# Adding the global keys' share of batch 0's first outputs by short matmuls from the picked rows, and sending those rows into the value tile by DMA

## The chip, the core and the metric

The kernel runs on one core of a Trainium2 chip. The metric is the device time of one execution, in microseconds (us). The kernel was already tuned: TensorE is busy in 97% of its span. A trace belongs to one execution. Traces start at the first instruction, so their spans are some 1.8 us shorter than the device times.

## The reference

Longformer attention, then a feed-forward block with a squared ReLU. Each query attends to the keys within 32 places of it and to eight global tokens; a global token attends to all and is attended by all.

```python
batch, n_heads, seq, head_dim = (8, 8, 576, 64); n_global = 8; window = 32
scores = scale * np.matmul(q, k.transpose(0, 1, 3, 2))
mask = (abs(pos[:, None] - pos[None, :]) <= window) | is_global[:, None] | is_global[None, :]
attn = softmax(np.where(mask, scores, -1e9))            # shortened
x = (attn @ v).transpose(0, 2, 1, 3).reshape(B * S, H * D)   # 4608 x 512
h = np.maximum(x @ w_in, 0.0)                            # w_in 512 x 2048
return (h * h) @ w_out                                   # w_out 2048 x 512
```

## The kernel before

The batches are worked through one after the other, and the expert matmuls (L543, L524 and L587, the two products of the feed-forward block) of one batch fill TensorE beside the attention of the next. Batch 0 has nothing to hide behind. Its heads are treated in four pairs, its 576 queries in two halves. A value tile `vb[b]` holds up to 120 keys in each of five tiles, and rows 0 to 7 of each tile are the eight global keys' values. For batch 0 these rows are picked from the tile itself with one-hot matrices `oh`, rounded to `gv16`, and copied into all five tiles before any output can be computed:

```python
def pick_values():
    gp = pst("mm", [P, 512])[0:NG]
    for x in range(NT):                                   # five matmuls of 512 columns
        nc.tensor.matmul(gp..., oh[:, x, :], vb[0][:, x, 0 : 2 * H : 2], start=(x == 0), stop=(x == NT - 1))
    dve.tensor_copy(out=gv16, in_=gp...)

def spread_values(b, op, tiles=range(NT)):
    for x in tiles:
        op(out=vb[b][0:NG, x, 0 : 2 * H : 2], in_=gv16)

# ... the program's order in batch 0, from the third pair's scores on
half0(2)                                                  # scores of pair 2, exponentials
half0(3)
pick_values()
spread_values(0, dve.tensor_copy, range(0, 4))
spread_values(0, act.copy, range(4, NT))
masked(0, ets[2], WIN)
masked(0, ets[3], WIN)
# ... DMAs of w_in, of batch 1 and of w_out; GpSimd's casts of global rows (next_in_place)
keep_warm(SCHED["w7"])                                    # four multiplications of zeros
half0_out(0, "mm"); half0_out(1, "sc"); half0_out(2, "acc"); half0_out(3, "mm")   # four lines in the file
```

`half0_out` computes a pair's outputs and denominators (L670), then `finish_outputs` takes Ln and Exp of the denominators on ScalarE (`rec`, L702 and L703) and multiplies on VectorE into `xT` (L732), which the expert matmuls read. After the four pairs come the first `scatter` of the global queries (L751), later the outputs of the second half, and a second scatter.

The softmax here doesn't subtract the row's maximum and nothing guards it: scores larger than these inputs give would overflow.

## Time and profile before

| | before |
|---|---|
| device time, median of 3 | 326.77 us (326.56 to 326.85) |
| profiled execution | 327.83 us, span 326.0 us |
| TensorE busy | 316.8 us, 2434 matmuls |
| first expert matmul starts | 25.79 us |
| clock granted to TensorE | 1.00 |

TensorE doesn't lose its clock once it has it: the page's line of the granted clock has a 9, the highest digit, in each of the forty slices of the span. (The line doesn't show the slow start: four zero matmuls at 3.47 us took 1.89 us, four at 17.08 took 1.04.) The lines of the chain and of TensorE's own timeline are in the prediction. One thing matters for all that follows: the profiled execution took 327.83 us, one microsecond over the median.

### The profile page before, as it was taken

The numbers are of one execution on the slowest core, as the hardware profiler recorded it, in microseconds if no ns is written. First come the engines' busy times: TensorE is split into PE (matmuls) and PEld (weight loads), VectorE is DVE, ScalarE is ACT, GpSimd is POOL, SyncE is SP. The second block draws the span as 40 slices with busy tenths as digits, with TensorE's granted clock in tenths as the row PEclk, the third lists the DMA queues.
The fourth block names the chain that finished last, engine by engine and source line by source line (L and its number), as shares of the span: only waits on it lengthen the run. The fifth ranks groups of instructions, "written<-read, shape, count | busy, mean of one in ns | idle before, by whom it ended". The sixth has DMA issues, their size and how long they took to land.

```text
span 326.0 us, 6920 instructions
## 1 busy us (share of the span) xinstructions
PE 316.8 (97%) x2434; PEld 164.5 (50%) x2434; DVE 227.0 (70%) x674; ACT 214.4 (66%) x418; POOL 110.2 (34%) x148
## 2 busy tenths in 40 slices
PE   6998999999999999999999999999999999999996
PEld 2645775445555455455545544454455544444444
DVE  7786987677878875987598758885888675313421
ACT  6677985569954995499549954995499636404600
POOL 9824663639800870089107700680000000000000
PEclk9999999999999999999999999999999999999999
DMA  8999999999994999399959996999610011011012
GB/s 186 176 204 190 174 186 167 154 147 107 153 131 141 73 138 171 134 83 139 132 162 82 148 126 144 98 134 132 139 60 0 34 58 39 2 73 56 2 54 75
DMA packets 148229, 37.53 MB, mean 115 GB/s; under 512 B 136171, under 2 KB 143715, under 8 KB 148195
## 3 DMA queue, kind: packets, MB, share of 16 engines
q0 software_dynamic: 105168, 17.93, 78.9%
q1 hardware_dynamic: 42880, 19.04, 30.3%
q8 instruction: 19, 0.31, 0.4%
q10 hardware_dynamic: 146, 0.13, 0.1%
q14 instruction: 16, 0.12, 0.1%
HBM read 37.30 MB, written 17.05 MB: 167 GB/s over the span
## 4 chain that ended last, share of the span: by engine, by line
PE 88%; DVE 7%; ACT 2%; issue 1%; DMA 1%
PE mm L587 29%; PE mm L524 26%; PE tr L524 9%; PE tr L587 7%; PE sc L679 3%; PE acc L679 3%; PE sc L627 3%; PE mm L543 2%; PE acc L627 2%; DVE xT L751 2%; PE tr L197 1%; DVE vb L457 1%; PE sc L670 1%; DVE xT L732 1%; ACT rec L702 1%
## 5 line engine op out<-in xcount | busy, mean ns | idle before, releaser
L587 PE MATMUL mm<-w_out,gt 128*128 128x512 f16 x448 | 104.4, 379 | 0.0
L524 PE MATMUL mm<-xT,w_in 128*128 128x512 f16 x384 | 90.8, 379 | 0.5 <-DVE xT L751 0.5
L587 PEld LDWEIGHTS <-gt 128*128 128x128 f16 x560 | 52.4, 98 | 58.6
L524 PEld LDWEIGHTS <-w_in 128*128 128x128 f16 x512 | 47.5, 98 | 53.7 <-issue 0.8
L529 ACT ACTIVATE rl<-mm 128x512 f16<-128x512 f32 x96 | 54.3, 599 | 26.7 <-PE mm L524 26.7
L530 DVE TENSOR_TENSOR gt<-rl 128x512 f16<-128x512 f16 x128 | 51.0, 422 | 17.0 <-ACT rl L529 15.6
L636 ACT ACTIVATE et<-sc 128x880 f16<-128x880 f32 (+1 forms) x32 | 29.0, 907 | 44.1 <-PE sc L627 39.1
L643 DVE TENSOR_TENSOR et<-et,mask 128x880 f16<-128x880 f16 (+1 forms) x64 | 38.9, 615 | 24.1 <-ACT et L636 23.8
L113 POOL DMA_DIRECT2D vb<-in_v_dram x40 | 40.7, 1532 | 9.0 <-DMA w_in<-in_moe_w_in_dram 7.3
L524 PE MATMUL tr<-xT,w_in 128*128 128x512 f16 x128 | 33.0, 380 | 0.0
L564 DVE COPY ot<-mm 128x512 f32<-128x512 f32 (+1 forms) x29 | 19.7, 680 | 18.0 <-PE mm L587 16.3
L636 ACT ACTIVATE et<-acc 128x880 f16<-128x880 f32 (+1 forms) x32 | 29.1, 909 | 1.0 <-PE acc L627 1.0
L703 ACT ACTIVATE rec<-rec 128x288 f32<-128x288 f32 x64 | 28.3, 443 | 2.0
L732 DVE TENSOR_TENSOR xT<-sc,rec 64x288 f16<-64x288 f32 (+1 forms) x55 | 25.0, 455 | 6.5 <-ACT rec L703 6.2
L732 DVE TENSOR_TENSOR xT<-acc,rec 64x288 f16<-64x288 f32 (+1 forms) x55 | 25.0, 455 | 3.9 <-ACT rec L703 1.1
L404 POOL DMA_DIRECT2D scr_k<-in_k_dram x30 | 26.6, 1111 | 2.8 <-issue 2.8
L679 PEld LDWEIGHTS <-vb 128*128 128x128 f16 x288 | 21.3, 98 | 11.5
L930 POOL COPY pin<-gsh 1x1 f32<-1x1 f32 x5 | 0.9, 177 | 76.4 <-DVE gsh L720 76.4
L702 ACT ACTIVATE rec<-sc 64x288 f32<-64x288 f32 (+1 forms) x55 | 22.3, 406 | 6.2 <-PE sc L679 4.2
L404 POOL DMA_DIRECT2D scr_q<-in_q_dram x24 | 25.1, 1585 | 3.0 <-DMA w_out<-in_moe_w_out_dram 3.0
L587 PE MATMUL tr<-w_out,gt 128*128 128x512 f16 x112 | 25.3, 379 | 0.0
L702 ACT ACTIVATE rec<-acc 64x288 f32<-64x288 f32 (+1 forms) x55 | 22.2, 404 | 2.0 <-PE acc L670 1.1
(147 smaller groups left out, 308.5 us busy)
## 6 DMA issues: line engine op xcount, KB each, us to landing
out_dram<-ot SPq DMA_DIRECT2D x35, 256.0 KB
vb<-in_v_dram POOLq DMA_DIRECT2D x32, 120.0 KB, 11.3
scr_q<-in_q_dram POOLq DMA_DIRECT2D x24, 144.0 KB, 5.9
scr_k<-in_k_dram POOLq DMA_DIRECT2D x24, 120.0 KB, 4.2
w_in<-in_moe_w_in_dram POOLq DMA_DIRECT2D x4, 512.0 KB, 11.9
w_out<-in_moe_w_out_dram POOLq DMA_DIRECT2D x4, 512.0 KB, 12.3
natk<-in_k_dram POOLq DMA_DIRECT2D x3, 288.0 KB, 10.9
natq<-in_q_dram POOLq DMA_DIRECT2D x3, 288.0 KB, 15.8
```

Of the source, the lines that this page charges most:

```text
L113: pool.dma_start(out=vb[b][NG : NG + KN[x], x, 2 * hs.start : 2 * hs.stop : 2], in_=v[b, hs, x * KT : x * KT + KN[x]].rearrange("h s d -> ...
L404: pool.dma_start(out=scr[(nm, b % 2)][x * pitch + off : x * pitch + off + hi - lo].rearrange("s (h d) -> s h d", d=D), in_=src[nm][b, :, l ...
L524: nc.tensor.matmul(ph, w_in[:, t, u * P : (u + 1) * P], xT[:, t, XOFF + c * TC : XOFF + (c + 1) * TC], start=(t == 0), stop=(t == NDM - 1),)
L529: nc.scalar.activation(out=rl, in_=ph, func=AF.Relu)
L530: nc.vector.tensor_tensor(out=gts[c][:, u, :], in0=rl, in1=rl, op=ALU.mult)
L587: nc.tensor.matmul(po, gts[c][:, f, m * P : (m + 1) * P], w_out[:, f, :], start=(f == 0), stop=(f == NFF - 1),)
L636: act.activation(out=et[:, :, 0:W], in_=sc[:, :, 0:W], func=AF.Exp, bias=0.0, scale=scale)
L643: dve.tensor_tensor(out=et[:, :, 0:W], in0=et[:, :, 0:W], in1=mask[:, MB[half] : MB[half] + W].unsqueeze(1).to_broadcast((P, 2, W)), op=AL ...
L679: nc.tensor.matmul(banks[e][:, o : o + w], vtf[:, t, vo : vo + P], et[:, e, so : so + w], start=(n == 0), stop=(n == nw - 1), skip_group_c ...
L702: act.activation(out=rec[r], in_=av[xs][rs, :, 0:GTOK], func=AF.Ln)
L703: act.activation(out=rec, in_=rec, func=AF.Exp, scale=-1.0)
L732: dve.tensor_tensor(out=xT[r, hp, x0 : x0 + HS].rearrange("p (k x) -> p k x", k=2), in0=av[x][r, :, 0:GTOK], in1=rec[r], op=ALU.mult,)
```

## The change

The intent is to take the copies of `gv16` out of the relay. The first half's outputs are computed from tiles whose rows 0 to 7 are still zero, and the global keys' share is added by 24 short matmuls that contract only the eight rows of `gv16`. The second half needs rows in tiles 2 to 4 alone, and gets them by three DMAs. Denominators don't need values, so pair 0's Ln may start before the share is added. The picks are split in two, and the first three windows of pair 0's outputs are put between the scores of pairs 2 and 3.

```diff
+    def pick_values(part):                    # half of the heads, 256 columns
...
+    def send_values():
+        for x in range(2, NT):
+            nc.sync.dma_start(out=vb[0][0:NG, x, 0 : 2 * H : 2], in_=gv16)
...
+    def global_keys(i, half, et, banks, wins):
...
+                nc.tensor.matmul(
+                    banks[0][D * e : D * e + D, lo_ - half * BANKC : hi_ - half * BANKC],
+                    gv16[:, 2 * hp + e], et[0:NG, e, off + lo_ : off + hi_],
+                    start=False, stop=(n == len(own) - 1), skip_group_check=True,
+                )
...
+    first = [pst("mm", [P, 512]), pst("tr", [P, 512])]
+    column_outputs(0, 0, ets[0], first, WIN, slice(0, 3))
     half0(3)
...
-    pick_values()
-    spread_values(0, dve.tensor_copy, range(0, 4))
-    spread_values(0, act.copy, range(4, NT))
     masked(0, ets[2], WIN)
-    masked(0, ets[3], WIN)
+    pick_values(0)
+    pick_values(1)
+    column_outputs(0, 0, ets[0], first, WIN, slice(3, None))
...
+    reciprocals(0, first, True)
+    second = output_banks("sc")
+    column_outputs(1, 0, ets[1], second, WIN, slice(None))
+    masked(0, ets[3], WIN)
+    global_keys(0, 0, ets[0], first, WIN)
+    global_keys(1, 0, ets[1], second, WIN)
...                                            # products of pairs 0 and 1, then all of pairs 2 and 3
+    send_values()
+    fetch_globals("v", at)                    # before: fetched with K and Q
     next_in_place()
-    keep_warm(SCHED["w7"])
```

The schedule's counts change with it: no zero matmuls in `w7`, one fewer in `wb`, `wc` and two fewer in `w`; two expert units (of eight matmuls) instead of one ahead of the second half's outputs, and one fewer before pair 3's second half. In the changed file the picks are L452, outputs L676, the new matmuls L697, Ln and Exp L741 and L742, the scatter L797, expert matmuls L550, L531 and L594.

More of the change, by code (lines that the diff above doesn't have):

```diff
@@ L42 @@
 MB = (0, 456)
-SCHED = dict(w8=2, w9=3, w5=3, w6=0, w7=4, wa=4, wb=3, wc=3, g0=1, w0=2, w1=4, w2=2, w3=2, w4=3, w=5, h0=0, h1=1, h4=1, h5=1, h2=1, h3=0, keep=1, b1=((3, 1, 3), (2, 1, 3), (2, 1, 3), (2, 1, 2)), last=((2, 1, 4), (3, 1, 4), (2, 1, 4), (2, 1, 7)))
+SCHED = dict(w8=2, w9=3, w5=3, w6=0, w7=0, wa=4, wb=2, wc=2, g0=2, w0=2, w1=4, w2=2, w3=2, w4=3, w=3, h0=0, h1=1, h4=1, h5=1, h2=0, h3=0, keep=1, b1=((3, 1, 3), (2, 1, 3), (2, 1, 3), (2, 1, 2)), last=((2, 1, 4), (3, 1, 4), (2, 1, 4), (2, 1, 7)))
 ONES = 2.0**-7 * (1.0 + 15360.0 / 2**23)
@@ L351, with fetch_globals @@
     g16s = {nm: sbt("g16s" + nm, [NG, H, D], FP16) for nm in "kqv"}
-    def fetch_globals():
-        _, at = nc.values_load_multi_w_load_instructions(
-            g32c[0:1, 0:NG], engines=[mybir.EngineType.SP], min_val=0, max_val=S - 1,
-            skip_runtime_bounds_check_because="the values are clamped on the chip",
-        )
-        for nm in "kqv":
+    def fetch_globals(names, at=None):
+        if at is None:
+            _, at = nc.values_load_multi_w_load_instructions(
+                g32c[0:1, 0:NG], engines=[mybir.EngineType.SP], min_val=0, max_val=S - 1,
+                skip_runtime_bounds_check_because="the values are clamped on the chip",
+            )
+        for nm in names:
             for g in range(NG):
@@ L363, in fetch_globals @@
                 )
+        return at
     def globals_in_place(nm):
@@ L444, in clear_value_rows @@
         )
-    def pick_values():
-        gp = pst("mm", [P, 512])[0:NG]
+    def pick_values(part):
+        gp = pst("mm", [P, 512])[0:NG, 0:256].rearrange("p (h d) -> p h d", d=D)
+        hs = slice(4 * part, 4 * part + 4)
         for x in range(NT):
             nc.tensor.matmul(
-                gp.rearrange("p (h d) -> p h d", d=D), oh[:, x, :], vb[0][:, x, 0 : 2 * H : 2],
+                gp, oh[:, x, :], vb[0][:, x, 8 * part : 8 * part + 8 : 2],
                 start=(x == 0), stop=(x == NT - 1),
             )
-        dve.tensor_copy(out=gv16, in_=gp.rearrange("p (h d) -> p h d", d=D))
+        dve.tensor_copy(out=gv16[:, hs], in_=gp)
+    def send_values():
+        for x in range(2, NT):
+            nc.sync.dma_start(out=vb[0][0:NG, x, 0 : 2 * H : 2], in_=gv16)
     def spread_values(b, op, tiles=range(NT)):
@@ L654, with output_banks, column_outputs @@
     PARTS = (((lo, 0, hi, 0), (hi, 1, lo, 1)), ((slice(0, P), 0, slice(0, P), 1),))
-    def outputs(i, half, et, tag, wins, columns=False):
-        b, hp = divmod(i, NHP)
-        if tag == "mm":
-            banks = [pst("mm", [P, 512]) for _ in range(2)]
-        else:
-            acc = pst(tag, [P, 2, 512])
-            banks = [acc[:, x] for x in range(2)]
-        vt = vb[b]
-        vtf = vt.rearrange("p t x d -> p t (x d)")
+    def output_banks(tag):
+        if tag == "mm":
+            return [pst("mm", [P, 512]) for _ in range(2)]
+        acc = pst(tag, [P, 2, 512])
+        return [acc[:, x] for x in range(2)]
+    def column_outputs(i, half, et, banks, wins, some):
+        b, hp = divmod(i, NHP)
         nw = len(wins[half])
-        for n, (t, so, c0, w) in enumerate(wins[half] if columns else ()):
+        for n, (t, so, c0, w) in list(enumerate(wins[half]))[some]:
             o = c0 - half * BANKC
@@ L671, in outputs @@
                         banks[x][D * e : D * e + D, o : o + w],
-                        one64 if x else vt[:, t, 4 * hp + 2 * e], et[:, e, so : so + w],
-                        start=(n == 0), stop=(n == nw - 1), skip_group_check=True,
-                    )
-        for e in () if columns else range(2):
+                        one64 if x else vb[b][:, t, 4 * hp + 2 * e], et[:, e, so : so + w],
+                        start=(n == 0), stop=(n == nw - 1 and (b + half > 0 or x > 0)),
+                        skip_group_check=True,
+                    )
+    def global_keys(i, half, et, banks, wins):
+        b, hp = divmod(i, NHP)
+        own = []
+        for t, so, c0, w in wins[half]:
+            cs = [
+                (max(KT * t + 8 * grp, GRP * grp, c0),
+                 min(KT * (t + 1) + 8 * grp, GRP * grp + GTOK, c0 + w))
+                for grp in range(4)
+            ]
+            cs = [c for c in cs if c[0] < c[1]]
+            if cs:
+                own.append((so - c0, cs[0][0], cs[-1][1]))
+        for n, (off, lo_, hi_) in enumerate(own):
+            for e in range(2):
+                nc.tensor.matmul(
+                    banks[0][D * e : D * e + D, lo_ - half * BANKC : hi_ - half * BANKC],
+                    gv16[:, 2 * hp + e], et[0:NG, e, off + lo_ : off + hi_],
+                    start=False, stop=(n == len(own) - 1), skip_group_check=True,
+                )
+    def outputs(i, half, et, tag, wins, columns=False):
+        b, hp = divmod(i, NHP)
+        banks = output_banks(tag)
+        if columns:
+            column_outputs(i, half, et, banks, wins, slice(None))
+            if b == 0 and half == 0:
+                global_keys(i, half, et, banks, wins)
+            return banks
+        vt = vb[b]
+        vtf = vt.rearrange("p t x d -> p t (x d)")
+        nw = len(wins[half])
+        for e in range(2):
             for n, (t, so, c0, w) in enumerate(wins[half]):
@@ L694, in global_outputs, with reciprocals @@
             )
+    recs = {}
+    def reciprocals(i, acc, columns):
+        rec = recs[i] = sbt("rec", [P, 2, GTOK], FP32, bufs=4)
+        for r, x, rs, xs in PARTS[columns]:
+            den = acc[xs][rs, 0:BANKC].rearrange("p (k c) -> p k c", c=GRP)
+            act.activation(out=rec[r], in_=den[:, :, 0:GTOK], func=AF.Ln)
+        act.activation(out=rec, in_=rec, func=AF.Exp, scale=-1.0)
     def finish_outputs(i, half, acc, columns=False):
@@ L699, in finish_outputs @@
         av = [a[:, 0:BANKC].rearrange("p (k c) -> p k c", c=GRP) for a in acc]
-        rec = sbt("rec", [P, 2, GTOK], FP32, bufs=4)
-        for r, x, rs, xs in parts:
-            act.activation(out=rec[r], in_=av[xs][rs, :, 0:GTOK], func=AF.Ln)
-        act.activation(out=rec, in_=rec, func=AF.Exp, scale=-1.0)
+        if i not in recs:
+            reciprocals(i, acc, columns)
+        rec = recs.pop(i)
         if b == 0:
@@ L712, in finish_outputs @@
                     )
-                if hp >= NHP - 2:
-                    a, z = (0, NHP - 1) if hp < NHP - 1 else (NHP - 1, NHP)
-                    global_outputs(0, gsum[0], a, z, columns)
+                if hp == NHP - 1:
+                    global_outputs(0, gsum[0], 0, NHP, columns)
         else:
@@ L765 @@
     gb = indices()
-    fetch_globals()
+    at = fetch_globals("kq")
     one_hots(gb)
@@ L784, in half0 @@
         ets[i] = exps(0, scores(i, 0, tag, WIN), WIN)
-    def half0_out(i, tag):
-        acc = outputs(i, 0, ets[i], tag, WIN, columns=True)
-        finish_outputs(i, 0, acc, columns=True)
     half0(0)
@@ L821 @@
         pool.dma_start(out=w_out[:, ts(j, 4), :], in_=wo[:, ts(j, 4), :])
-    next_in_place()
-    keep_warm(SCHED["w7"])
-    half0_out(0, "mm")
-    half0_out(1, "sc")
-    half0_out(2, "acc")
-    half0_out(3, "mm")
+    reciprocals(0, first, True)
[4 more added lines that the diff above has]
+    global_keys(1, 0, ets[1], second, WIN)
+    finish_outputs(0, 0, first, columns=True)
+    finish_outputs(1, 0, second, columns=True)
+    for i, tag in ((2, "acc"), (3, "mm")):
+        finish_outputs(i, 0, outputs(i, 0, ets[i], tag, WIN, columns=True), columns=True)
+    send_values()
+    fetch_globals("v", at)
+    next_in_place()
     def half1(i):
```

## The prediction

> **What bounds the kernel now.** I read the page first, the chain that ended last:
>
> ```profile
> PE 88%; DVE 7%; ACT 2%; issue 1%; DMA 1%
> ```
>
> TensorE carries 88% of the span. So I asked for the same chain in order of time and for busy time in stretches of 5 us. From about 46 us on, TensorE is busy without a gap, but for 0.51 us before 69.50, and that part the change leaves alone. Only before 46 us do other engines carry the chain. The change lies in 15 to 26 us. Columns of the chain: start, length, what.
>
> ```profile
> 14.80 0.64 ACT qt L506
> ...
> 15.58 0.40 PE acc L627 x9
> 15.97 1.19 PE mm L449 x5
> ...
> 17.18 0.69 DVE gv L453
> ...
> 17.90 1.33 DVE vb L457 x4
> ...
> 19.27 0.32 PE mm L670 x8
> ...
> 19.62 0.42 ACT rec L702
> ...
> 22.85 0.17 DVE gs L709 x2
> ...
> 23.04 0.21 DVE gr L690
> ...
> 23.36 0.46 DVE xT L732
> ...
> 23.85 0.19 DVE xT L751
> ```
>
> This is a relay. The picks of the global value rows (L449) wait behind the last scores; VectorE rounds them (gv) and copies them into the value tile (vb, x4); only then do the first half's outputs finish (L670). Four rounds of Ln and Exp on ScalarE and the products xT follow, and the scatter of the global queries (L751, eight copies to 25.75). TensorE in order of time shows what it does meanwhile (the bracket is idle time and who ended it):
>
> ```profile
> 15.58 0.40 PE L627 MATMUL acc<-qt,kt 64*128 64x160 f16 x10 [0.49 <-ACT qt L510]
> ...
> 17.08 1.04 PE L197 MATMUL tr<-idle 128*128 128x512 f16 x4
> ...
> 19.27 0.20 PE L670 MATMUL mm<-et,vb 128*64 128x8 f16 x2 [0.36 <-DVE vb L457]
> ...
> 23.38 1.25 PE L197 MATMUL tr<-idle 128*128 128x512 f16 x5
> 25.79 1.03 PE L543 MATMUL mm<-xT,w_in 128*128 128x256 f16 x8 [1.16 <-DVE xT L751]
> ```
>
> It idles 0.49, 0.36 and 1.16 us and fills the rest with multiplications of zeros (L197). The first useful expert matmul starts at 25.79. If the relay ends earlier, all that follows starts earlier, unless a transfer holds it. The GpSimd queue, which waits for landings, tells when those are:
>
> ```profile
> 26.60 0.90 POOL L113 DMA_DIRECT2D vb<-in_v_dram  x1 [1.48 <-DMA w_in<-in_moe_w_in_dram]
> ...
> 29.63 0.79 POOL L821 DMA_DIRECT2D w_out<-in_moe_w_out_dram  x1 [0.40 <-DMA natq<-in_q_dram]
> ...
> 48.38 1.79 POOL L404 DMA_DIRECT2D scr_q<-in_q_dram  x2 [1.66 <-DMA w_out<-in_moe_w_out_dram]
> ```
>
> [...] I read these as the last quarter of w_in landed by 26.60, batch 1's first queries by 29.63, the last quarter of w_out by 48.38.
>
> [...] the trace's gv cast took 679. [...] ten half picks cost TensorE what five whole ones did. [...] two scatter copies that meet GpSimd's casts (36.07 to 37.22) took 0.64 and 0.53 us, the others 0.19. [...] landings of the small queue-SP transfers are not shown in this trace.
>
> **The change part by part.** I take the relay's times from before and replay the changed order of each engine's queue, which I compared by building both.
>
> 1. Head start of the first pair. Three windows of pair 0's outputs move between the scores of pairs 2 and 3. From 19.42 to 19.83 such windows took about 0.4 to 0.5 us, so they fit into the 0.49 us idle before 15.58. The last scores still start near 15.6, the picks near 16.0, ending at 17.1.
> 2. Denominators no longer wait for values. They need the weights and ones only. After the picks come eight 8-column matmuls (0.15 us as at 19.27 to 19.42, latency 0.17), so Ln of pair 0 starts at about 17.4 instead of 19.62: 2.2 us earlier. The four vb copies (1.33 us) and ScalarE's (0.62) leave the path.
> 3. The cadence. Ln plus Exp took 0.78 us a pair (19.62, 20.41, 21.18, 21.95). TensorE must keep pace: pair 1's outputs to 17.7, then the new matmuls from the picked rows. These are 24 matmuls, per pair (120+128+48) columns for two heads side by side; 160 columns for two heads took about 0.07 us, so 0.13 to 0.15 us a pair, 0.6 us in all, beside ScalarE's work. They need gv16: VectorE masks pair 2 (16.4 to 17.0), [...] masks pair 3 (to 18.4). Pair 2's outputs end at 18.6, pair 3's at 19.3, each before its Ln. Reciprocals are ready at about 18.3, 19.0, 19.8, 20.6 (before: 20.5, 21.3, 22.05, 22.8).
> 4. VectorE's tail. gs, gr and gx are no longer split 3+1: one gr of 32 elements, about 0.35 us from 303 ns for 24 and 203 for 8. From pair 2's product at 19.9: product 0.4, gs 0.2, gr 0.35, gx 0.2, so pair 3's product starts at about 21.0 (before 23.36), the scatter at 21.5, its end at 23.4 (before 25.75). GpSimd's issue at 24.23, which lengthened one copy to 0.42, falls outside. **TensorE's first expert matmul moves from 25.79 to about 23.4: 2.35 us.**
> 5. Up to there TensorE has less filler (9 zero matmuls instead of 16). It idles about 1.5 us before 23.4, short; I expect no loss of clock.
> 6. Afterwards. Two expert units instead of one come first, and one fewer before pair 3's second half; one zero matmul less (0.22). Pair 2's outputs come 0.76 us later after the new start than after the old; ScalarE then does Ln, Exp, the query copies, Ln, Exp without the 0.6 us Relu between. Pair 3's reciprocal is ready 0.25 us later relative to the start. So of 2.35, about 2.1 us is left at the second scatter, which 38.59 waited for. From there to 45.1 VectorE carries the chain, and GpSimd's three casts (35.5 to 37.2, tied to landings that do not move) now meet the scatter's end and the following products instead of its start: plus or minus 0.3; I take -0.1.
>
> Sum: 2.35 - 0.25 - 0.1 = 2.0 us, and 326.77 - 2.0 = 324.7 us.
>
> **Rivals.**
>
> - *The value rows by DMA arrive late.* The queue issues them after pair 3's last reading (about 19.3), at 0.7 us each as the five like it at 60.94 took 3.99 us; so the last is issued at 21.4 [...]. The first reading is at 23.4 + 1.96 = 25.4, behind two expert units. The 16 DMA engines are full there, so a landing near 26.5 is possible: the gain falls to 1 us or 1.5, 325.3 to 325.8. That two units were put in front speaks for a wait that was seen and hidden.
> - *Landings become the bound.* Batch 1's queries (29.63) are needed at about 30.5, w_out's last quarter (48.38) at about 50.4, batch 1's last value tile (about 40, estimated from the 1.5 us spacing of landings) at 40.3. All just pass. If one fails by half a microsecond: 325.2.
> - *Nothing is gained, since VectorE carries 36 to 45 us anyway.* Against it: its start there is set by pair 3's outputs, which move with TensorE. That would give 326.5.
> - *A larger gain*, if the relay shortens as told and GpSimd's casts miss the scatter: up to 0.5 more, 324.1.
> - *Slower*, if global rows for K and Q waited for those of V, now fetched later (issued 21 to 27 us): ScalarE would stall some 5 us, 329. The separate waits of each copy in the built program speak against it.
>
> **Range and chances.** The mechanism rests on one long serial stretch with measured durations; the uncertainty is what is lost after it, 0 to 1.2 us, and up to 0.7 us more of gain. So 323.9 to 325.7. Two per cent is 6.5 us, more than the idle and filler there could give: same is nearly certain.
>
> **What would show it.** Right: the first Ln near 17.4, the first expert matmul near 23.4, no gv-to-vb copy before it, the new matmuls about 0.6 us in all, the wait for the second scatter still there (0.6 to 1 us) and ended near 36.5. Wrong: a TensorE wait for a DMA before the second half's first output; a clock below 1.0; Ln of pairs 1 to 3 waiting for TensorE.

The sum is 2.35 - 0.25 - 0.1 = 2.0 us as it stands, since the forecast kept the casts beside ScalarE's rounds and the flight belongs to a rival. In step 3 the end of pair 3's mask (18.4) and of the outputs of pairs 2 and 3 (18.6 and 19.3) rest on the length of the casts.

Some things are estimates of mine. That ten half picks cost what five whole ones do was measured only later (1.25 us in e3, 1.24 in before). The landing near 26.5 was a guess with no measured flight behind it (from 23.4 to 26.5 us before's DMA engines moved 205 GB/s). That 1.5 us of idle time cost no clock wasn't shown either; from 15 to 26 us before's trace has waits of 0.49, 0.36 and 1.16 us, at full clock. The quarters are read from the order on the GpSimd queue of that trace: its sixteenth to nineteenth transfers wait for the landings of the eighth to eleventh, the four quarters of w_in.

## The result, and the profile after

| | before | after |
|---|---|---|
| device time, median of 4 | 326.81 us (326.56 to 327.78) | 331.07 us (330.52 to 332.07) |
| ratio | | 1.0128, 95% interval 1.0095 to 1.0161 |
| clock of the four executions | 1.0 in the profiled one | 0.984 to 0.990 |

The change makes the kernel 1.3% slower, where 0.6% faster was predicted. A ratio here is always the mean time of one kernel's fast runs over the mean of the other's in the same rounds, so it is not quite the ratio of the medians quoted.

The page of the kernel after, the clock line (forty slices of the span, tenths of full speed) and the chain's shares by engine:

```profile
PEclk9978999999999999999999999999999999999999
...
PE 91%; DVE 4%; DMA 2%; issue 1%; ACT 1%
```

VectorE's share of the chain fell from 7% to 4%, as intended, but two slices of the span have a lower clock, and DMA holds a larger share. The chain of the kernel after in order of time (start, length, what):

```profile
14.65 0.40 PE acc L634 x9
15.05 2.23 issue
17.29 2.22 PE mm L452 x10
...
24.43 6.28 DMA vb<-gv
```

Three things are new. TensorE stands still for 2.23 us before the picks, and the view gives "issue", which means that the engine waited for nothing the profile shows. The picks then take 2.22 us instead of 1.19. And a sent value row takes 6.28 us to land. TensorE's timeline of the same kernel (start, time, operation, count; idle time before and who ended it in the bracket) has the same three, with what they did to the expert matmuls:

```profile
17.29 2.22 PE L452 MATMUL mm<-vb,oh 128*8 128x256 f16 x10 [2.25 <-issue]
...
26.74 1.91 PE L550 MATMUL mm<-xT,w_in 128*128 128x256 f16 x16 [1.00 <-DVE xT L797]
...
30.75 0.25 PE L676 MATMUL sc<-et,vb 128*64 128x136 f16 x2 [1.62 <-DMA vb<-gv]
...
32.81 1.83 PE L550 MATMUL mm<-xT,w_in 128*128 128x256 f16 x8
```

Eight expert matmuls took 1.83 us here, and 1.05 in the next two units. Busy times by stretches of 4 us (columns: TensorE, its weight loads, VectorE, ScalarE and GpSimd, then the granted clock, the mean DMA occupation and GB/s) show the clock behind both stops:

```profile
18.00:22.00 4.00, 4.00 (x76) 3.05 (x75) 2.20 (x8) 1.59 (x4) 1.66 (x2) 0.65 1.25 207
...
30.00:34.00 4.00, 3.25 (x24) 1.83 (x25) 0.61 (x2) 1.70 (x4) 1.64 (x3) 0.63 2.80 136
```

These two shares are averages. The trace's clock records have exactly half clock from 17.40 to 20.81 us and from 31.05 to 34.46, 3.41 us each, and full clock between. The same view, cut at these times, for the first stop:

```profile
13.99:17.40 3.41, 1.16 (x34) 1.04 (x29) 1.13 (x6) 2.26 (x4) 1.85 (x3) 1.00 1.28 204
17.40:20.81 3.41, 3.41 (x42) 2.37 (x42) 1.36 (x3) 0.85 (x2) 1.57 (x2) 0.50 1.25 206
```

For a fair difference, I use the second trace of the kernel before (span 324.9 us, run e10 below), since the first was a late execution. Its TensorE timeline, the first outputs (behind four zero matmuls that start at 16.20) and the first expert matmuls:

```profile
17.35 0.26 PE L670 MATMUL mm<-et,vb 128*64 128x160 f16 x2
...
24.59 1.03 PE L543 MATMUL mm<-xT,w_in 128*128 128x256 f16 x8 [1.27 <-DVE xT L751]
```

The first expert matmul is 26.74 - 24.59 = 2.15 us later in the kernel after. The wait for the DMA adds 1.62 and the slow expert unit 1.83 - 1.05 = 0.78: 4.55 us together. The second scatter ends 4.73 us later (42.29 against 37.56), and the spans differ by 5.4. So the loss is made before 43 us, and its larger part is the three items above. The remaining 0.7 us I did not trace. (The changed kernel's trace is of its slowest execution, 332.07 us; the means of the two kernels' executions are 4.2 us apart, not 5.4.)

The traces also show the position of the stop. Counted from the span's start to just before it (the same view of busy times, kernel after), TensorE had done 222 matmuls and 223 weight loads:

```profile
0.00:17.10 17.10, 13.59 (x222) 8.29 (x223) 12.29 (x56) 11.62 (x23) 14.04 (x31) 1.00 1.34 183
```

And between 14 and 18 us the DMA view of this kernel lists, beside the two data queues (queue: packets, MB, share of 16 engines), one packet of instructions:

```profile
q8 instruction: 1, 0.02, 1.5%
```

In the trace's DMA records it starts at 14.85 us and takes 0.96. Over the whole span this queue moves 19 packets, 0.31 MB, and each has 16384 bytes in those records. TensorE's 2455 matmuls and as many loads are 4910 instructions, 258 to a packet (an estimate: 4910 / 19, if all the packets are TensorE's). So I read the queue as TensorE's instruction stream, fetched in blocks of some 256 instructions; e2 below shows a second stop after exactly 256 more.

**My theory** was therefore: TensorE reaches the end of what has been fetched, at its 446th instruction, before the next block is there; the stop costs clock; and the late DMA costs a second stop and clock again. **The rivals:** the picks wait for some data the profile doesn't show (they read all the value tiles); the stop is a bystander and the DMA is the whole loss; or only the loss of clock counts, so that filler in the stop repairs it.

### The profile page after: what moved, and what is told of

It is laid out like the page before. It is cut to its first block, busy times and chain, and to the rows that moved or that the text cites. A ratio compares the mean times of both kernels' runs of the same rounds, so it can differ in the third digit from the quotient of the medians.

```text
span 330.3 us, 6962 instructions
## 1 busy us (share of the span) xinstructions
PE 319.4 (97%) x2455; PEld 167.1 (51%) x2455; DVE 225.7 (68%) x669; ACT 214.2 (65%) x417; POOL 110.5 (33%) x148
## 2 busy tenths in 40 slices
DMA packets 148444, 37.56 MB, mean 114 GB/s; under 512 B 136386, under 2 KB 143930, under 8 KB 148410
## 4 chain that ended last, share of the span: by engine, by line
PE 91%; DVE 4%; DMA 2%; issue 1%; ACT 1%
PE mm L594 29%; PE mm L531 25%; PE tr L531 9%; PE tr L594 7%; PE sc L718 3%; PE acc L718 3%; PE sc L634 3%; PE tr L197 2%; PE mm L550 2%; DMA vb<-gv 2%; PE acc L634 2%; DVE xT L797 1%; PE sc L676 1%; PE acc L676 1%; PE mm L477 1%
## 5 line engine op out<-in xcount | busy, mean ns | idle before, releaser
L594 PE MATMUL mm<-w_out,gt 128*128 128x512 f16 x448 | 104.4, 379 | 0.0
L531 PE MATMUL mm<-xT,w_in 128*128 128x512 f16 x384 | 90.8, 379 | 0.6 <-DVE xT L797 0.6
L594 PEld LDWEIGHTS <-gt 128*128 128x128 f16 x560 | 52.4, 98 | 58.5
L531 PEld LDWEIGHTS <-w_in 128*128 128x128 f16 x512 | 47.5, 98 | 53.8 <-issue 0.9
L531 PE MATMUL tr<-xT,w_in 128*128 128x512 f16 x128 | 32.9, 380 | 0.0
L742 ACT ACTIVATE rec<-rec 128x288 f32<-128x288 f32 x64 | 28.3, 443 | 2.0
L741 ACT ACTIVATE rec<-sc 64x288 f32<-64x288 f32 (+1 forms) x55 | 22.3, 406 | 8.1 <-PE sc L718 4.2
L594 PE MATMUL tr<-w_out,gt 128*128 128x512 f16 x112 | 25.3, 379 | 0.0
L741 ACT ACTIVATE rec<-acc 64x288 f32<-64x288 f32 (+1 forms) x55 | 22.3, 405 | 2.4 <-PE acc L676 1.5
```

The lines of the kernel that those rows point to most:

```text
L531: nc.tensor.matmul(ph, w_in[:, t, u * P : (u + 1) * P], xT[:, t, XOFF + c * TC : XOFF + (c + 1) * TC], start=(t == 0), stop=(t == NDM - 1),)
L594: nc.tensor.matmul(po, gts[c][:, f, m * P : (m + 1) * P], w_out[:, f, :], start=(f == 0), stop=(f == NFF - 1),)
L741: act.activation(out=rec[r], in_=den[:, :, 0:GTOK], func=AF.Ln)
L742: act.activation(out=rec, in_=rec, func=AF.Exp, scale=-1.0)
```

## The experiments

Twelve runs were made, in three batches, each batch on one chip with runs of the kernel before beside it (medians of before: 326.40, 327.26 and 326.62 us). All gave correct results.

| run | built on | median us | ratio to before | 95% interval |
|---|---|---|---|---|
| e1 | after | 329.32 | 1.0077 | 1.0019 to 1.0135 |
| e2 | after | 329.58 | 1.0083 | 1.0053 to 1.0113 |
| e3 | after | 328.50 | 1.0073 | 1.0028 to 1.0118 |
| e4 | before | 329.87 | 1.0104 | 1.0072 to 1.0137 |
| e5 | after | 326.85 | 0.9994 | 0.9980 to 1.0007 |
| e8 | after | 327.24 | 1.0005 | 0.9991 to 1.0019 |
| e7 | after | 332.05 | 1.0149 | 1.0130 to 1.0167 |
| e9 | before | 327.74 | 1.0011 | 0.9996 to 1.0027 |
| e9b | before | 329.01 | 1.0065 | 1.0027 to 1.0103 |
| e10 | before, unchanged | 326.44 | 0.9986 | 0.9956 to 1.0017 |
| e11 | after | 325.67 | 0.9967 | 0.9946 to 0.9989 |
| e12 | before | 326.39 | 0.9984 | 0.9957 to 1.0011 |

**e1: VectorE copies in place of the DMAs.** The three sends are undone, and VectorE copies tiles 2 to 4 after the second half's first masks.

```diff
-    send_values()
...
     masked(1, ets[1], WIN2)
+    spread_values(0, dve.tensor_copy, range(2, NT))
```

> The changed kernel with one part undone: the picked rows go into value tiles 2 to 4 by three VectorE copies after the masks of the second half's first two pairs, not by DMA. Theory A (the DMA landed 6.3 us after its issue; TensorE waited 1.62 us for it and then ran some 3 us at half clock): no wait before the third window of the second half's first output, clock 1.0 from 26 to 34 us, 2.5 to 3 us off, so about 328.3 us. Rival B (the loss of that stretch lies in the new order or comes back in VectorE): 0.5 us off or less, 330.5 or more. Under both, the 2.25 us gap before the picks stays.

Median 329.32 us, ratio 1.0077 instead of 1.0128: some 0.5%, or 1.7 us, less, where 2.5 to 3 us had been expected; the two intervals overlap, so the times alone don't resolve the size. The trace does show the effect: no wait for `vb<-gv` is left. The other stop stayed where it was (TensorE's timeline of e1):

```profile
17.33 2.29 PE L452 MATMUL mm<-vb,oh 128*8 128x256 f16 x10 [2.35 <-issue]
```

So the DMA is one cause, and not the whole loss. The four executions differ by what happened to the clock: 327.09 us with a clock of 1.0, 328.43 (the traced one, with one stretch of 3.41 us at half clock) with 0.995, 330.21 and 330.35 with 0.984. A mean clock of 0.984 over the span is worth about three such stretches (an estimate: 0.016 x 328 us, doubled, is 10.5 us), which here took 3.2 us together. So the larger part of e1's loss goes with the clock: the execution that kept it is 0.4 us above the mean of before in its batch (326.65). Whether that untraced execution had the stop isn't known.

**e2: 32 tiny matmuls ahead of everything concerned.** If the stop hangs on the count of instructions, 64 more of them (a load and a matmul each) move it 64 instructions upstream; if it hangs on the picks' data, it stays at the picks.

```diff
     keep_warm(SCHED["w1"])
+    tiny(32)                      # matmuls of 8 columns on zeros
```

> The changed kernel with 32 tiny matmuls (64 TensorE instructions, 8 columns each) added near 4 us, where TensorE has time. Theory F (the 2.25 us gap is TensorE waiting for its next block of 256 instructions, whose fetch passes through full DMA engines): the gap moves 64 instructions forward in the program, off the picks and in front of the first scores of pair 2, and the picks follow their predecessors at once. Rival W (the picks wait for the value tiles' DMA or for a PSUM bank): the gap stays right before the picks. Time within 1 us of the changed kernel under both, 330 to 332.

Median 329.58 us. The stop left the picks. Instruction 446 now lay in the scores of pair 2, which started at 16.87 us without a stop. A new one came further on (TensorE's timeline of e2, then its counts up to there):

```profile
23.46 0.32 PE L702 MATMUL mm<-et,gv 8*64 8x120 f16 x6 [1.55 <-issue]
```

```profile
0.00:23.30 23.30, 20.41 (x350) 13.67 (x351) 15.15 (x68) 14.92 (x31) 15.86 (x33) 1.00 1.31 189
```

That is 701 instructions, against 445 in the kernel after: 256 more, one block. A position that moves with the count, and reappears after exactly one more block, speaks for the fetch and against any data. But my assumption that tiny matmuls are free was wrong: they took 1.8 us on TensorE's path, 57 ns each, and in e4, which has them at the same place, the delay grew. So the time of this run tests nothing.

**e3: the first windows put back behind the picks.** This undoes the head start only.

```diff
-    first = [pst("mm", [P, 512]), pst("tr", [P, 512])]
-    column_outputs(0, 0, ets[0], first, WIN, slice(0, 3))
...
-    column_outputs(0, 0, ets[0], first, WIN, slice(3, None))
+    first = [pst("mm", [P, 512]), pst("tr", [P, 512])]
+    column_outputs(0, 0, ets[0], first, WIN, slice(None))
```

> The changed kernel with the first three windows of pair 0 put back behind the picks. Theory F: the picks now lie before the block boundary and run at about 15.1 us without a gap; the gap comes behind them, in front of the first output matmuls of pair 0 (445th row), up to about 17.3; gv16 is ready 2 us earlier, first Ln near 18.4 instead of 19.86, 0.5 to 1.5 us off: 329.6 to 330.6. Rival W: the gap stays in front of the picks, and the time stays or grows.

Median 328.50 us, ratio 1.0073 (again with an interval that overlaps the changed kernel's). The picks, now twelve matmuls earlier in the count, ran at 14.76 us without a stop, and the stop fell into the outputs (TensorE's timeline of e3):

```profile
16.97 0.26 PE L676 MATMUL tr<-et,one 128*64 128x160 f16 x1 [0.70 <-issue]
```

Counts up to there: 223 matmuls and 223 loads. So it is the same instruction number in another operation. As the picks are done by the time of the stop, it is 0.70 us instead of 2.25, no clock is lost in this trace, and the first expert matmul starts at 23.92 us. The rows are still sent by DMA here, and TensorE waits for them twice, 0.30 and 0.65 us.

**e4: the kernel before with the same 32 tiny matmuls.**

```diff
     keep_warm(SCHED["w1"])
+    tiny(32)
```

> The kernel before with the same 32 tiny matmuls near 4 us. Theory F: it gets a gap that it doesn't have, up to about 1.5 us in front of the first scores of pair 2 (near 14.7 us), and the time grows by 0.5 to 1.5 us: 327.3 to 328.3. Rival W: no gap, time within 0.2 us of the kernel before.

Median 329.87 us, 1.0% slower, and no stop. The size was missed, again because the tiny matmuls themselves delay everything behind them, by 1.9 us at first (6.12 us instead of 4.25 in e10) and by 3.1 at the picks (18.13 instead of 15.02). In between TensorE ran at half pace for longer: three zero matmuls at 10.75 us took 1.41 us, the same three in e10, at 8.23, took 0.82. So TensorE reached instruction 446 at about 17 us, when the block was there. Inconclusive.

**e5: e1 and e3 together.** Copies on VectorE, and the picks ahead of the windows.

> The changed kernel with both repairs: picks before the first outputs, and the second half's value rows copied by VectorE instead of sent by DMA. Theories A and F together: a gap of some 0.7 us at the 446th TensorE instruction, no wait for the rows, first expert matmul near 24 us, and no clock drop in most runs: 326 to 327.3 us, level with the kernel before (326.4). If it stays at 328 or more, something else in the new order costs time.

Median 326.85 us, ratio 0.9994: level with before. So undoing these two parts takes away the whole loss of 1.3%. (Alone they took away 0.5% and 0.55%; given their intervals, whether the two together do more than the sum isn't resolved.) The trace keeps a stop of 0.61 us at instruction 446 and a clock of 1.0, and the first expert matmul starts at 23.55. The gain that is left upstream doesn't reach the end. VectorE's timeline of e5 shows the second scatter, and GpSimd's the first of its three casts (two views of one kernel):

```profile
33.89 2.77 DVE L797 COPY xT<-gx 128x4 f16 x8
```

```profile
34.69 0.60 POOL L372 CAST g16sk<-grows 8x512 f16<-8x512 f32 x1
```

The other two casts follow without a pause, to 36.4. Of the eight scatter copies the three that started during the casts took 0.47, 0.54 and 0.53 us; one before them, beside a DMA issue of GpSimd (33.89 to 34.64), took 0.31, the others 0.19. TensorE waited 1.12 us for this scatter.

**e8: e5 with two zero matmuls behind the picks.** This tests whether filler in the stop is free, and whether it matters.

```diff
+    keep_warm(2)
     first = [pst("mm", [P, 512]), pst("tr", [P, 512])]
```

> As e5_both, with two 512-column matmuls of zeros behind the picks, where TensorE would wait for its next block anyway. Theory F: they cost nothing (0.43 us inside the 0.7 us gap; the boundary then falls on the first output matmul), and keep the clock up: within 0.4 us of e5_both or a little faster, 325.8 to 327. Rival (TensorE's order is bound by work, not by the block): 0.4 us slower than e5_both.

Median 327.24 us, ratio 1.0005, 0.4 us above e5 with overlapping intervals. The filler shortened the stop only from 0.61 to 0.39 us and moved its end from 16.89 to 17.22; 0.16 of these 0.33 us is the instruction packet, which was later in this trace. So it was not shown to be free, and the rival of this run isn't excluded. With the clock at 1.0 in both, filling has nothing to repair, and the rival that only the clock counts stays untested here; e1's executions speak for its larger part.

**e7: the kernel after, 20 tiny matmuls in place of two zero matmuls.** These lie at the start, where TensorE has idle time, and add 36 instructions without a delay. This is e2 without its flaw.

```diff
-    keep_warm(SCHED["w0"])
+    tiny(20)
```

> The changed kernel with 20 tiny matmuls in place of the first two of zeros, in the first 2.4 us, when TensorE waits for the indices: 36 instructions more, no time. Theory F: the gap moves 36 instructions forward and falls inside the first windows of pair 0 (at the 446th row, a matmul of 192 columns from the value tile), about 2 us long; the picks follow their predecessors without a gap. Rival W: the gap stays in front of the picks. Time 330 to 332 under both.

Median 332.05 us (two runs). The stop sits again behind 222 matmuls and 223 loads, this time in the first windows of pair 0; the picks, behind it, ran without one (TensorE's timeline of e7):

```profile
17.00 0.27 PE L681 MATMUL mm<-et,vb 128*64 128x192 f16 x2 [1.84 <-issue]
```

**e9 and e9b: the same edit in the kernel before,** run twice. If the count is all, before can be given the stop.

> The kernel before with the same 20 tiny matmuls in the first 2.4 us: 36 instructions more, no time. Theory F: the boundary (446th row) moves from the first outputs, which it reaches only after 17 us, into the scores of pair 3 (near 14.7 us); it gets a gap of about 2 us there, which the relay passes on: 328 to 329.5 us. Rival W: no gap, within 0.3 us of the kernel before.

> The kernel before with 20 tiny matmuls early, once more: its first trace (331.16 us) had the gap and a clock at half for some 4 us, its four other executions were at 327.35 to 327.74. Theory F: the gap of about 1.7 us at the 446th row is there again; with the clock up the time is 327.3 to 328, with the clock down 330.5 to 331.5. If there is no gap at 327.6 us, the fetch is late only in some executions.

The profiled execution of e9 took 331.16 us, as slow as the change, and has the stop in the scores of pair 3, after 223 matmuls and 223 loads (TensorE's timeline of e9):

```profile
16.72 0.28 PE L632 MATMUL acc<-qt,kt 64*128 64x88 f16 x5 [1.68 <-issue]
```

Behind it the clock was 0.50 from 17 to 22 us. So the kernel before, with nothing of the change in it, loses the same time in the same way in this execution. But the other four executions of e9 took 327.35 to 327.74, about 0.4 us more than before, where 328 to 329.5 had been expected. (The ratio in the table leaves the profiled execution out; the mean of all five is 0.34% above before's.) And the profiled execution of e9b (328.03 us; its other one took 329.99, with a clock of 0.993) has no stop: its instruction packet started at 13.28 us, over a microsecond earlier than in e9 (14.48), and TensorE came to instruction 446 at 16.36 us instead of 14.84. It was late because it ran at half pace for longer near the start: two zero matmuls took 1.03 us at 7.44, in e9 0.60 at 7.36, and three took 1.46 at 8.92, in e9 0.82 at 8.23. From these two traces, whether a kernel stops there is a race between two times, and it isn't lost in each execution.

**e10: the kernel before, traced again.**

> The kernel before itself, for a second trace: in the first one the indices landed at 2.84 us, in the traces of the other kernels near 2.0. Theory F: here too TensorE reaches its 446th row (the first outputs of pair 0) only after its block is there, at about 17.3 us, so no gap or one under 0.3 us. Time as the kernel before, 326.3 to 327.4; first expert matmul 0 to 1 us earlier than 25.79.

326.65 us in the profiled execution, 24.59 us for the first expert matmul, and no stop. By 17.30 us it had done 219 matmuls and 219 loads; the four zero matmuls and the wait for the copies bring it to instruction 446 at 17.4 us, about when the block can be used. So the relay that the change shortened seems to have hidden the fetch.

Over the runs with a stop at instruction 446, its end follows the instruction packet's end (starts from the DMA records, plus 0.96 us):

| run | idle before it | packet ends | TensorE resumes | difference |
|---|---|---|---|---|
| after | 2.25 us | 15.81 | 17.29 | 1.48 |
| e1 | 2.35 | 15.86 | 17.33 | 1.47 |
| e3 | 0.70 | 15.65 | 16.97 | 1.32 |
| e5 | 0.61 | 15.61 | 16.89 | 1.28 |
| e8 | 0.39 | 15.77 | 17.22 | 1.45 |
| e7 | 1.84 | 15.70 | 17.00 | 1.30 |
| e9 | 1.68 | 15.44 | 16.72 | 1.28 |
| e11 | 0.64 | 15.62 | 16.96 | 1.34 |

The second stop of e2, one block later, ends 1.68 us after its packet (21.78, then 23.46). So nine of the fourteen traces have such a stop, of 0.39 to 2.35 us.

**e11: e5 with GpSimd's casts moved away from the scatter.** The rows of V are fetched with K and Q as before, and the casts are issued ahead of the loads of w_out.

```diff
-    at = fetch_globals("kq")
+    at = fetch_globals("kqv")
...
+    next_in_place()
     for j in range(4):
         pool.dma_start(out=w_out[:, ts(j, 4), :], in_=wo[:, ts(j, 4), :])
```

> As e5_both (picks first, VectorE copies), with GpSimd's three casts moved ahead of the w_out loads, out of the second scatter, which took 2.77 us in e5_both as against 1.65 where no cast met it. Theory: the second scatter takes 1.6 to 2.0 us, 0.5 to 1 us off e5_both: 0.2 to 0.4% faster than the kernel before. Rival (contention only moves to other VectorE work, or the loads of w_out come too late): level with e5_both, ratio 0.998 to 1.001.

Median 325.67 us, ratio 0.9967 with an interval below one. The second scatter (VectorE's timeline of e11):

```profile
34.03 1.83 DVE L797 COPY xT<-gx 128x4 f16 x8
```

It took 1.83 us instead of 2.77, and TensorE's wait for it is gone. This version beats the kernel before by 0.3%, and so the changed one too. Its interval overlaps that of e5, so what the moved casts alone add is seen in the scatter, but not resolved in the times.

**e12: only the casts moved, in the kernel before.**

```diff
+    next_in_place()
     for j in range(4):
         pool.dma_start(out=w_out[:, ts(j, 4), :], in_=wo[:, ts(j, 4), :])
-    next_in_place()
```

> The kernel before with the same move of the three casts alone. If the casts alone make the gain: 0.3 to 0.6 us faster than before (two scatter copies lost 0.8 us to them), ratio 0.998 to 0.999. If it needs the earlier start as well: ratio 0.999 to 1.001.

Median 326.39 us, ratio 0.9984, an interval that holds one. The second scatter is short here too (1.66 us), but the time is not resolved from before's. So e11's gain is the shortened relay and the moved casts together; how it divides between them isn't settled.

## Why the prediction was wrong

**Step 1, "The last scores still start near 15.6, the picks near 16.0", is the step that failed.** The three windows did fit where I put them (14.08 to 14.61 us, the scores of pair 3 at 14.64). But the picks started 2.25 us after TensorE had nothing to wait for. I had counted data and engines, and had taken it that an instruction in the program is at hand when its turn comes. The runs put in its place: TensorE stops after 445 or 446 instructions, whichever operation that is (picks in after and e1, outputs in e3, e5, e8 and e11, windows in e7, the kernel before's scores in e9), and in e2 after 256 more. That the position goes with the count is shown. That the missing instructions are the cause is inferred from the packets, whose ends precede the resumption by 1.28 to 1.48 us in eight traces (1.68 at e2's next block). What makes the block be asked for at about 14.7 us, and why TensorE needs 1.3 us and more after its packet, isn't in the traces.

**Step 2**, Ln of pair 0 at "about 17.4 instead of 19.62", fell with it: 19.86. Its base was also too high. In the second trace of before this Ln starts at 18.30, because TensorE and ScalarE were about a microsecond earlier there and the four copies took 0.89 us and not 1.33. So there were fewer microseconds to win than the one late trace promised. In e5 it starts at 17.53.

**Step 3** was nearly right in its pieces. The casts of `gv16` took 0.41 us each. The new matmuls took 0.25 us on the chain for each of pairs 2 and 3, where I had 0.13 to 0.15, and 0.9 us in all instead of 0.6. Ln plus Exp took 0.79 to 0.90 us a pair in e5, not 0.78.

**Step 4** was right in its mechanism: one reciprocal of 32 elements took 0.35 us as estimated, and from the first Ln to the first expert matmul e5 needs 23.55 - 17.53 = 6.02 us, where the prediction has 23.4 - 17.4 = 6.0. That the sums agree so well is partly luck: the last product starts 3.82 us after the first Ln, not 3.6, and the scatter behind it took 1.66 us, not 1.9. The 23.4 itself came out as 26.74 in the changed kernel, and as 23.55 to 23.95 once the picks were put ahead of the windows.

**Step 5, "I expect no loss of clock", failed** as a consequence of step 1. I had looked at the idle time before the expert matmuls only. The clock was at half for 3.41 us behind each of the changed kernel's two stops. At that clock the ten picks took 0.21 us each instead of the half of 0.24 that I assumed; at full clock the assumption holds (ten took 1.25 us in e3, five whole ones 1.24 before). With the stop kept short the clock was 1.0 in the traces of e3, e5, e8 and e11.

The length of a stop alone doesn't tell whether the clock falls. The stop of 1.84 us in e7 cost none (1.00 from 14 to 27 us), nor did that of 1.55 us in e2 (1.00 from 14 to 38), but e7's DMA wait of 1.67 us did (0.58 from 30 to 34), and e9's stop of 1.68. The half clock lasted 3.41 us, or 6.83 in e9, so I counted TensorE's idle time in the 3.41 us just before it: 2.25 and 1.62 us in after, 1.94 in e1, 1.67 in e7, 1.53 in e9. In stretches of 3.41 us counted back from e7's half clock, its stop of 1.84 us falls into two, as 1.15 and 0.69. That the stretches are what decides is my reading of these five cases.

**Step 6** named GpSimd's casts against the second scatter and gave them 0.1 us, plus or minus 0.3. That term was mis-sized for the repaired kernel: eight copies took 2.77 us in e5 and 1.83 in e11. In the changed kernel as given the casts did not meet the scatter at all, since everything had become later (eight copies in 1.65 us).

**The rivals.** "The value rows by DMA arrive late" came true and larger than told: I had a landing "near 26.5" as the bad case, and it was 30.71. The issue that the chain follows starts at 24.43, where I had the last one at 21.4, and the flight took 6.28 us, for 8 KB within SBUF on the sync engine's queue, while the DMA engines moved 197 GB/s. As the prediction says, before's trace didn't show such landings. The issues were also misread: five in 3.99 us are 0.8 us each, not 0.7, and the three took 2.53. e1 puts the cost of the sends at some 1.7 us, with the doubt told there. The landings of weights and of batch 1, and ScalarE waiting for K and Q, were not seen to bind.

So the mechanism of the gain existed and was worth about a microsecond at the first expert matmul (24.59 in e10, 23.62 in e11, on one chip). The prediction listed a clock below 1.0, a DMA wait among the second half's first outputs and an Ln that waits for TensorE as signs of its failure, and all three appeared (the Ln of pair 1 waited 0.48 us).

## What to carry to other kernels

When a change makes an engine reach a place in its program earlier, ask what else had to be ready by then besides data. Here the likeliest answer is its own instructions, which, as these traces are read above, arrive by DMA too (a packet of 16384 bytes ended 1.28 to 1.48 us before TensorE went on), and idle "issue" time at a fixed instruction count, whatever stands there, was the mark of it. Keep serial work that others depend on ahead of such a place (e3), and keep a small transfer off the path while the DMA engines are busy (8 KB took 6.28 us at 197 GB/s) if a free engine can copy the rows (e1, e5). Stops of 0.4 to 0.7 us (e3, e5, e8, e11) cost no clock in the traces; those of 2.25 and 2.35 us did, and between 1.55 and 1.84 us it went both ways. Take a second trace before resting sums of tenths on the first: here it was a microsecond late in the very part that mattered.
